# Where a matrix's operand words are cut in the queue of a seven-product gated MLP kernel

## The chip, the cores and the metric

The kernel runs on one core of one Trainium2 chip. The metric is the device time of one execution in microseconds (us); the kernel before takes 1533.95 us, the median of three runs.

## The reference

The program normalises `x` (2048 x 576), runs a linear attention on it and a gated MLP beside it, and returns `x + s * silu(MLP)`. The change touches only the first part of the MLP:

```python
def _B_ref(x, w_gate, w_up, w_down):
    g = jnp.einsum("bsd,df->bsf", x, w_gate)      # 2048 x 576 x 4608
    u = jnp.einsum("bsd,df->bsf", x, w_up)
    h = _gelu(g) * u
    return jnp.einsum("bsf,fd->bsd", h, w_down)
```

All arrays are float32.

## The kernel before, in words

The two products with `w_gate` and `w_up` are cut into 36 *matrices*, q = 0 to 35. An even q is a block of 256 columns of `w_gate`, an odd q the same columns of `w_up`; the two together are called a pair here. Each matrix is a 2 x 2 block product done with seven products instead of eight. `STEPS` lists them in the order in which TensorE (PE) does them: k = 0 to 6 with the weights A11, S1, S3, S2, A12, S4, A22. S1 to S4 are sums of the four weight blocks: S1 = A21 + A22, S2 = S1 - A11, S3 = A11 - A21, S4 = A12 - S2. GpSimd (POOL) makes all four per matrix in `mat_sums`, into the tile `sm`.

Every product is done for two halves s of the tokens, s = 1 first. Float32 accuracy comes from two float32r words per value, so each sum and each raw block is cut into words: `cut_w` has ScalarE (ACT) copy the high word and then VectorE (DVE) subtract it twice (the low word of 2 x 128 rows, then that of a group of 32 rows). In the profile these are ACT `wa<-sm`, `wb<-raw` and so on at L104, and two DVE subtractions of the same names at L107. `wa` holds the words of A11, S1, S2, S3, `wb` those of A12, A22, S4.

The products add into PSUM banks named `al`, `ga`, `de`, `be`; (k - q) % 4 chooses the bank, so the next matrix takes each bank over in turn: `be` of matrix q+1 takes the bank of `de` of matrix q, `al` that of `be`, `ga` that of `al`, `de` that of `ga`. PE works on four groups of 32 rows, each group running some steps behind the group before it, so PE starts a bank of the next matrix about 3.5 us after the last matmul of this matrix into that bank. In between, DVE or ACT must have read it out.

The order on DVE, ACT and POOL is the order in which the program is written; an instruction that waits holds all behind it on its engine. `roll` emits the matmuls, and behind the last of a step (q, k, s) it calls `matrix(...)`'s `step`, which reads the bank. Behind step k with s = 0 it runs the list `todo[k]`. That list comes from `mat_pieces(q + 1)`, so the words of the next matrix are cut in the shadow of this one:

```python
            if s == SBS[-1]:
                run(todo[k])
```

An up matrix (odd q) multiplies the hidden tile `h` by what the banks give (DVE) and has POOL make eight sums of hidden blocks (`hs`, `h`) that go to DRAM. A gate matrix (even q) passes each block through a Gelu on ACT, and `down_sums` behind its k = 3 has POOL make four sums of the down weights (`td`). POOL takes up the four sums `sm` for the next matrix behind step k = 0.

The MLP's second part (`down_all`, L1068), the attention before it and all loads stay as they are.

Of the kernel before, what the change touches and what calls it, by code (L numbers as in the profile page):

```python
# [57 lines left out]
def group(t):  # L58
    return slice(t * KR, (t + 1) * KR)
# [6 lines left out]
def block_kernel(ctx, tc, x, xe, xt_d, wq_d, wkv0_d, wkv1_d, wkv2_d, wo, wgu_d, wd_d, out):  # L66
# [22 lines left out]
    def mid(i, shape, dt, name):  # L89
        return sb.tile(shape, dt, tag=f"m{i}", bufs=1, name=name)  # L90
# [12 lines left out]
    def act(*args, **kw):  # L103
        pin(nc.scalar.activation(*args, **kw))  # L104

    def vec(op, *args, **kw):
        pin(getattr(nc.vector, op)(*args, **kw))  # L107
# [6 lines left out]
    def pool(op, *args, **kw):  # L114
        pin(getattr(nc.gpsimd, op)(*args, **kw))
# [370 lines left out]
    def run(todo, n=None):  # L486
        for _ in range(len(todo) if n is None else min(n, len(todo))):
            todo.pop(0)()
# [243 lines left out]
    def s_mm(tb, t):  # L732
# [15 lines left out]
        if t == 0:  # L748
# [6 lines left out]
    raw, sums, wt = {}, {}, {}  # L755
# [3 lines left out]

    W_AT = {"A11": ("a", 0), "S1": ("a", 1), "S2": ("a", 2), "S3": ("a", 3),
            "A12": ("b", 1), "S4": ("b", 3)}

    def w_at(q, nm):
        t, i = ("b", 2 if q % 2 == 0 else 0) if nm == "A22" else W_AT[nm]
        return wt[t][:, i]

    def load_mat(q):
        if q < NQ:  # L770
            raw[q] = mid(0, [P, 2, 3, 2 * P], F32, f"raw_{q}")
            dma(out=raw[q], in_=wgu_d[q // 2, q % 2])

    def mat_sums(q):
        if q >= NQ:
            return
        rv = raw[q].rearrange("p j k (f c) -> p j f k c", f=2)
        a11, a21, a12, a22 = rv[:, 0, 0], rv[:, 0, 1], rv[:, 1, 0], rv[:, 1, 1]
        sm = mid(2, [P, 4, 3, P], F32, f"sm_{q}")
        pool("tensor_add", sm[:, 0], a21, a22)  # L780
        pool("tensor_sub", sm[:, 1], sm[:, 0], a11)
        pool("tensor_sub", sm[:, 2], a11, a21)
        pool("tensor_sub", sm[:, 3], a12, sm[:, 1])
        sums[q] = rv, sm

    def cut_w(o, src, nm):

        r = group(W_LO[nm])
        act(o[:, :, 0:3, :], src, AF.Copy)
        vec("tensor_sub", o[:, :, 3:5, :], src[:, :, 0:2, :], o[:, :, 0:2, :].bitcast(F32))  # L790
        vec("tensor_sub", o[r, :, 2, :], src[r, :, 2, :], o[r, :, 2, :].bitcast(F32))

    def mat_pieces(q):

        if q >= NQ:
            return [[] for _ in range(7)]
        rv, sm = sums.pop(q)
        if q % 2 == 0:
            raws_ = [lambda: cut_w(wt["b"][:, 1:3], rv[:, 1], "A12")]
        else:  # L800
            raws_ = [
                lambda: cut_w(wt["b"][:, 1:2], rv[:, 1, 0:1], "A12"),
                lambda: cut_w(wt["b"][:, 0:1], rv[:, 1, 1:2], "A22"),
            ]
        return [
            [lambda: cut_w(wt["a"][:, 0:1], rv[:, 0, 0:1], "A11")],
            [], [],
            [lambda: cut_w(wt["a"][:, 1:4], sm[:, 0:3], "S1")],
            raws_,
            [lambda: cut_w(wt["b"][:, 3:4], sm[:, 3:4], "S4")],  # L810
            [],
        ]

    STEPS = (
# [570 lines left out]
    def back(*names, eng=nc.gpsimd):  # L1385
        for nm in names:
            X[0][nm] = big(X_BACK[nm], [P, 5, TBN], F32R, f"xr_{nm}")
            dma(X[0][nm].bitcast(F32), store[0, nm], eng)

    def first_matrix():  # L1390
        wt["a"] = big(15, [P, 4, 5, P], F32R, "wa")
        return mat_pieces(0)
# [11 lines left out]
        (3, 2): [lambda: scale(0, 2, 3, 4), lambda: halve(0, 2, 3, 4)],  # L1404
        (3, 3): [lambda: build(1, "T4", X_SLOT["T4"]), lambda: back("T2")],
        (0, 0): [lambda: den(1), lambda: mat_sums(0)],
        (0, 1): [lambda: scale(1, 0, 1), lambda: halve(1, 0, 1)],
        (0, 2): [lambda: scale(1, 2, 3, 4), lambda: halve(1, 2, 3, 4)],
        (0, 3): [lambda: back("T1")],
        (1, 0): [lambda: pieces.extend(first_matrix()), lambda: run(pieces[0])],  # L1410
        (1, 1): [lambda: run(pieces[3])],
    }
    pieces = []
    for tb in (2, 3, 0, 1):
# [2 lines left out]
            run(aside.get((tb, t), []))  # L1417
    wt["b"] = big(14, [P, 4, 5, P], F32R, "wb")
    back("T3")
    run(pieces[4] + pieces[5])  # L1420
    load_mat(1)
    back("B21", "B22", "T4", eng=nc.sync)

    def matrix_of(q):

        g = q // 2
        mat_sums(q + 1)
        todo = mat_pieces(q + 1)
        if q % 2 == 0:
            todo[0].append(lambda: load_down(g))  # L1430
            todo[3].append(lambda: down_sums(g))
        todo[4].append(lambda: load_mat(q + 2))
        if q == NQ - 1:
            load_s(3)
            todo[0].append(lambda: load_t(1))
            todo[2].append(lambda: prep_t(1))
            todo[3] += [lambda: load_t(2), lambda: prep_s(1)]
            todo[4].append(lambda: prep_s(2))
            todo[4].append(lambda: load_s(5))
            todo[5].append(lambda: load_t(3))  # L1440
            todo[6].append(lambda: prep_s(3))
        return (gate_matrix if q % 2 == 0 else up_matrix)(g, todo)
# [59 lines left out]
```

## Time and profile before

| | before |
|---|---|
| runs, us | 1533.95, 1532.64, 1534.01 |
| profiled execution, us | 1536.59 |
| its span, us | 1534.5 |
| PE busy | 1484.4 us, 97% |
| DVE busy | 1063.6 us, 69% |
| ACT busy | 604.9 us, 39% |
| POOL busy | 548.1 us, 36% |
| 333 to 1112 us (the pairs): PE, DVE, POOL busy | 740.4, 589.9, 398.8 of 779.0 us |

The granted TensorE clock is 0.997 over the span, and 1.00 in the stretch of the pairs. In a row of the profile the first number is the start in us, the second the length, then engine, line, operation, out<-in, shapes; what stands in square brackets is the engine's idle time before the instruction and what ended it. Names lack their numbers, so `u<-u,de` is the DVE sum of `u` and the bank `de` for whichever matrix and half.

### The profile page before, as it was taken

How to read it: one execution, taken by the hardware profiler on the slowest of the kernel's cores; microseconds unless marked ns; L12 is line 12 of the kernel's file. 1: busy time of each engine (PE TensorE's matmuls, PEld its weight loads, DVE VectorE, ACT ScalarE, POOL GpSimd, SP SyncE). 2: the span in 40 equal slices, each digit the busy share in tenths (PEclk: the TensorE clock that was granted, in tenths of full speed). 3: DMA queues.
4: the chain of work that ended last, by engine and by line, in shares of the span. 5: the costliest groups of instructions: out<-in, count | busy, mean ns of one | idle time of the engine just before them, and what ended most of it. 6: DMA issues, size and time to landing. Idle time of an engine off the chain costs nothing.

```text
span 1534.5 us, 42454 instructions
## 1 busy us (share of the span) xinstructions
PE 1484.4 (97%) x18431; PEld 1392.7 (91%) x18431; DVE 1063.6 (69%) x1579; ACT 604.9 (39%) x1119; POOL 548.1 (36%) x520
## 2 busy tenths in 40 slices
PE   9999999999999999999999999999999999999998
PEld 8989989988888888888889888889889999999998
DVE  7676567277778777778777778777684666555775
ACT  5444455333332233332233332233334545444443
POOL 5452521144565544565544565544410020000120
PEclk9999999999999999999999999999989999999999
DMA  6354015633344333344423443423577757787773
GB/s 231 128 219 163 1 52 193 247 126 117 135 170 164 140 120 115 142 170 150 153 103 125 150 169 145 156 99 123 211 286 245 255 169 249 245 267 250 277 244 126
DMA packets 114548, 261.96 MB, mean 171 GB/s; under 512 B 10218, under 2 KB 38634, under 8 KB 112314
## 3 DMA queue, kind: packets, MB, share of 16 engines
q1 hardware_dynamic: 112586, 249.95, 46.0%
q0 software_dynamic: 1632, 8.91, 1.6%
q8 instruction: 144, 2.36, 0.7%
q14 instruction: 42, 0.34, 0.1%
q10 hardware_dynamic: 144, 0.39, 0.1%
HBM read 161.27 MB, written 97.91 MB: 169 GB/s over the span
## 4 chain that ended last, share of the span: by engine, by line
PE 70%; DVE 25%; issue 2%; ACT 1%; DMA 1%; SPq 0%; ACTq 0%
PE bd L1068 26%; PE be L110 9%; DVE h L107 8%; PE kv L110 7%; PE de L110 7%; PE al L110 7%; DVE wb L107 7%; DVE u L107 6%; PE ga L110 5%; PE s L110 3%; PE q L110 3%; DVE wa L107 3%; PE kv_a L110 1%; ACT wa L104 1%; DMA x<-in_xe_dram 0%
## 5 line engine op out<-in xcount | busy, mean ns | idle before, releaser
L1068 PE MATMUL bd<-t,s 128*128 128x288 f32 x3024 | 405.6, 296 | 3.5 <-DVE u L107 3.5
L1068 PEld LDWEIGHTS bd<-t,s 128*128 128x128 f32 x3024 | 404.8, 189 | 4.5 <-DVE u L107 4.1
L110 PE MATMUL be<-xo_T,wa 32*128 32x512 f32 x972 | 248.0, 389 | 28.6 <-DVE u L107 28.6
L110 PE MATMUL de<-xo_T,wa 32*128 32x512 f32 x972 | 255.9, 393 | 10.0 <-DVE h L107 9.9
L107 DVE TENSOR_TENSOR s<-sr,s 128x512 fp32r<-128x512 f32 x252 | 176.0, 739 | 125.0 <-ACT s L104 120.5
L110 PE MATMUL al<-xr_B,wa 32*128 32x512 f32 x972 | 256.6, 391 | 0.0
L110 PE MATMUL ga<-xr_T,wa 32*128 32x512 f32 x972 | 252.4, 390 | 0.0
L110 PE MATMUL ga<-xo_T,wa 32*128 32x512 f32 x972 | 252.4, 390 | 0.0
L110 PE MATMUL de<-xr_T,wb 32*128 32x512 f32 x972 | 248.9, 387 | 0.0
L110 PE MATMUL de<-xr_T,wa 32*128 32x512 f32 x972 | 246.9, 387 | 0.0
L110 PE MATMUL be<-xr_T,wa 32*128 32x512 f32 x972 | 245.4, 386 | 0.0
L110 PE MATMUL al<-xo_B,wa 32*128 32x512 f32 x972 | 245.1, 386 | 0.0
L110 PE MATMUL ga<-xr_B,wb 32*128 32x512 f32 x972 | 244.0, 385 | 0.0
L110 PE MATMUL de<-xo_T,wb 32*128 32x512 f32 x972 | 243.4, 384 | 0.0
L110 PE MATMUL al<-xo_B,wb 32*128 32x512 f32 x972 | 243.4, 384 | 0.0
L110 PE MATMUL al<-xr_B,wb 32*128 32x512 f32 x972 | 243.1, 384 | 0.0
L110 PE MATMUL ga<-xo_B,wb 32*128 32x512 f32 x972 | 243.0, 384 | 0.0
L104 ACT ACTIVATE s<-sr 128x512 fp32r<-128x512 f32 x252 | 148.7, 625 | 195.7 <-PE bd L1068 149.1
L110 PEld LDWEIGHTS be<-xo_T,wa 32*128 32x128 f32 x972 | 175.1, 183 | 46.9 <-DVE u L107 35.8
L110 PEld LDWEIGHTS de<-xo_T,wa 32*128 32x128 f32 x972 | 172.6, 183 | 22.1 <-DVE h L107 17.2
L110 PEld LDWEIGHTS be<-xr_T,wa 32*128 32x128 f32 x972 | 176.4, 183 | 10.9 <-DVE u L107 5.5
L110 PEld LDWEIGHTS de<-xr_T,wa 32*128 32x128 f32 x972 | 176.4, 183 | 5.6
(177 smaller groups left out, 4318.6 us busy)
## 6 DMA issues: line engine op xcount, KB each, us to landing
sr<-hs SPq DMA_DIRECT2D x252, 256.0 KB
hs<-h SPq DMA_DIRECT2D x68, 512.0 KB
raw<-in_wgu_dram SPq DMA_DIRECT2D x36, 768.0 KB
hs<-hs SPq DMA_DIRECT2D x102, 256.0 KB
td<-in_wd_dram SPq DMA_DIRECT2D x18, 576.0 KB
td<-td SPq DMA_DIRECT2D x18, 576.0 KB
tr<-td SPq DMA_DIRECT2D x16, 576.0 KB
tr<-in_wd_dram SPq DMA_DIRECT2D x12, 576.0 KB
```

The lines of the kernel that those rows point to most:

```text
L104: pin(nc.scalar.activation(*args, **kw))
L107: pin(getattr(nc.vector, op)(*args, **kw))
L110: i = nc.tensor.matmul(*args, **kw)
L1068: nc.tensor.matmul(banks[j][:, 0:HALF], hw[n, s][:, a, t * P : (t + 1) * P], w[:, c, g % 4], start=(new and g == 0 and m == 0), stop=(g == ...
```

## The change

The words of S1 and S3 are cut behind the third product (k = 2) and no longer behind the fourth; those of S2 stay behind the fourth (k = 3), now alone; those of S4 go from behind the sixth (k = 5) to behind the last (k = 6). So that S1 and S3 lie side by side, S3 and S2 change places in `wa` and in `sm`, and POOL makes S3 before S2.

```diff
-    W_AT = {"A11": ("a", 0), "S1": ("a", 1), "S2": ("a", 2), "S3": ("a", 3),
+    W_AT = {"A11": ("a", 0), "S1": ("a", 1), "S3": ("a", 2), "S2": ("a", 3),
...
         pool("tensor_add", sm[:, 0], a21, a22)
-        pool("tensor_sub", sm[:, 1], sm[:, 0], a11)
-        pool("tensor_sub", sm[:, 2], a11, a21)
-        pool("tensor_sub", sm[:, 3], a12, sm[:, 1])
+        pool("tensor_sub", sm[:, 1], a11, a21)
+        pool("tensor_sub", sm[:, 2], sm[:, 0], a11)
+        pool("tensor_sub", sm[:, 3], a12, sm[:, 2])
...
             [lambda: cut_w(wt["a"][:, 0:1], rv[:, 0, 0:1], "A11")],
-            [], [],
-            [lambda: cut_w(wt["a"][:, 1:4], sm[:, 0:3], "S1")],
+            [],
+            [lambda: cut_w(wt["a"][:, 1:3], sm[:, 0:2], "S1")],
+            [lambda: cut_w(wt["a"][:, 3:4], sm[:, 2:3], "S2")],
             raws_,
-            [lambda: cut_w(wt["b"][:, 3:4], sm[:, 3:4], "S4")],
             [],
+            [lambda: cut_w(wt["b"][:, 3:4], sm[:, 3:4], "S4")],
```

The first matrix, whose words are cut ahead of `roll`, takes its pieces by the new numbers (`pieces[2] + pieces[3]`, `pieces[4] + pieces[6]`); the order there is the same.

DVE's queue at the end of an up matrix (q = 11; `wb<-sm` are the words of S4 for matrix 12, `u_1`, `u_0` with `de` the reading of the last product). Before:

```order
L107 TENSOR_TENSOR u_5_0_8434<-u_0_8124,ga_0_8009 128x512
L107 TENSOR_TENSOR h_0_1_7655<-h_0_1_7655,u_5_0_8434 128x512
L107 TENSOR_TENSOR wb<-sm_8088,wb 128x256
L107 TENSOR_TENSOR wb<-sm_8088,wb 32x128
L107 TENSOR_TENSOR u_1_8093<-u_1_8093,de_1_8040 128x512
L107 TENSOR_TENSOR h_1_0_7652<-h_1_0_7652,u_1_8093 128x512
L107 TENSOR_TENSOR u_0_8124<-u_0_8124,de_0_8071 128x512
L107 TENSOR_TENSOR h_0_0_7654<-h_0_0_7654,u_0_8124 128x512
L107 TENSOR_TENSOR wa<-raw_8363,wa 128x256
```

Now:

```order
L107 TENSOR_TENSOR u_5_0_8473<-u_0_8160,ga_0_8042 128x512
L107 TENSOR_TENSOR h_0_1_7688<-h_0_1_7688,u_5_0_8473 128x512
L107 TENSOR_TENSOR u_1_8129<-u_1_8129,de_1_8073 128x512
L107 TENSOR_TENSOR h_1_0_7685<-h_1_0_7685,u_1_8129 128x512
L107 TENSOR_TENSOR u_0_8160<-u_0_8160,de_0_8107 128x512
L107 TENSOR_TENSOR h_0_0_7687<-h_0_0_7687,u_0_8160 128x512
L107 TENSOR_TENSOR wb<-sm_8124,wb 128x256
L107 TENSOR_TENSOR wb<-sm_8124,wb 32x128
L107 TENSOR_TENSOR wa<-raw_8402,wa 128x256
```

The two subtractions of S4 have gone behind the four instructions that read `de`.

DVE's queue in the middle of a gate matrix (q = 12; `wa<-sm` are the words for matrix 13, `u_1`, `u_0` with `be` the reading of the fourth product, `wb<-raw` the words of the next A12). Before:

```order
L107 TENSOR_TENSOR h_0_1_8555<-h_0_1_8555,de_0_8526 128x512
L107 TENSOR_TENSOR u_1_8556<-u_1_8556,be_1_8566 128x512
L107 TENSOR_TENSOR h_1_1_8553<-h_1_1_8553,u_1_8556 128x512
L107 TENSOR_TENSOR u_0_8587<-u_0_8587,be_0_8598 128x512
L107 TENSOR_TENSOR h_0_1_8555<-h_0_1_8555,u_0_8587 128x512
L107 TENSOR_TENSOR wa<-sm_8547,wa 128x3x256
L107 TENSOR_TENSOR wa<-sm_8547,wa 32x3x128
L107 TENSOR_TENSOR wb<-raw_8363,wb 128x256
```

Now:

```order
L107 TENSOR_TENSOR h_0_1_8594<-h_0_1_8594,de_0_8565 128x512
L107 TENSOR_TENSOR wa<-sm_8586,wa 128x2x256
L107 TENSOR_TENSOR wa<-sm_8586,wa 32x2x128
L107 TENSOR_TENSOR u_1_8595<-u_1_8595,be_1_8605 128x512
L107 TENSOR_TENSOR h_1_1_8592<-h_1_1_8592,u_1_8595 128x512
L107 TENSOR_TENSOR u_0_8626<-u_0_8626,be_0_8637 128x512
L107 TENSOR_TENSOR h_0_1_8594<-h_0_1_8594,u_0_8626 128x512
L107 TENSOR_TENSOR wa<-sm_8586,wa 128x256
L107 TENSOR_TENSOR wa<-sm_8586,wa 32x128
L107 TENSOR_TENSOR wb<-raw_8402,wb 128x256
```

Two of the three sums' words now stand ahead of the reading of `be`, as two instructions of their own; up matrices change in the same way. DVE and ACT have 72 and 36 rows more in all; SP's and PE's queues are in the same order as before.

More of the change, by code (lines that the diff above doesn't have):

```diff
@@ L806, in mat_pieces @@
             [lambda: cut_w(wt["a"][:, 0:1], rv[:, 0, 0:1], "A11")],
-            [], [],
-            [lambda: cut_w(wt["a"][:, 1:4], sm[:, 0:3], "S1")],
+            [],
+            [lambda: cut_w(wt["a"][:, 1:3], sm[:, 0:2], "S1")],
+            [lambda: cut_w(wt["a"][:, 3:4], sm[:, 2:3], "S2")],
             raws_,
+            [],
             [lambda: cut_w(wt["b"][:, 3:4], sm[:, 3:4], "S4")],
-            [],
         ]
@@ L1410, in block_kernel @@
         (1, 0): [lambda: pieces.extend(first_matrix()), lambda: run(pieces[0])],
-        (1, 1): [lambda: run(pieces[3])],
+        (1, 1): [lambda: run(pieces[2] + pieces[3])],
     }
@@ L1419, in block_kernel @@
     back("T3")
-    run(pieces[4] + pieces[5])
+    run(pieces[4] + pieces[6])
     load_mat(1)
```

## The prediction

> **What bounds the kernel now.** I read the page first, then PE's waits, and then the timelines of one pair, engine by engine. PE is busy 97% of the span, so only its idle time can be won, and PE's waits between 325 and 1112 us, where the pairs run, name all of that but refill:
>
> ```profile
> PE be L110 <- DVE u L107: 28.6, 17, 1.7
> PE de L110 <- DVE h L107: 9.9, 16, 1.2
> ```
>
> Two waits repeat, once a pair: 1.7 us before `be` of a gate matrix and 0.6 us on average before `de` of an up matrix. The pair of matrices 12 (gate) and 13 (up) stands for the rest. First PE, two rows of its timeline, the first matmuls of two neighbouring steps:
>
> ```profile
> 565.83 0.38 PE L110 MATMUL de<-xr_T,wa 32*128 32x512 f32 x1
> ...
> 569.30 0.49 PE L110 MATMUL be<-xo_T,wa 32*128 32x512 f32 x1 [1.66 <-DVE u L107]
> ```
>
> This step takes 3.47 us. A step without a wait takes 1.48 (2.95 for two, from the rows at 581.85 and 584.80 below), so the stall costs 2.0, some 0.3 more than its gap. What DVE did before it:
>
> ```profile
> 553.16 0.69 DVE L107 TENSOR_TENSOR u<-u,de 128x512 f32<-128x512 f32 x1 [0.90 <-PE de L110]
> 554.47 0.69 DVE L107 TENSOR_TENSOR u<-u,be 128x512 f32<-128x512 f32 x1 [0.61 <-PE be L110]
> ...
> 558.58 1.52 DVE L107 TENSOR_TENSOR wa<-sm,wa 128x768 fp32r<-128x768 f32 x2
> ...
> 561.33 1.12 DVE L107 TENSOR_TENSOR wb<-raw,wb 128x512 fp32r<-128x512 f32 x2
> ...
> 564.53 1.28 DVE L107 TENSOR_TENSOR h<-h,u 128x512 f32<-128x512 f32 x1
> 565.73 2.79 DVE L107 TENSOR_TENSOR wb<-sm,wb 128x256 fp32r<-128x256 f32 x2
> 568.55 0.69 DVE L107 TENSOR_TENSOR u<-u,de 128x512 f32<-128x512 f32 x1
> ```
>
> The words of S4 (565.73) hold DVE for 2.79 us, and `u<-u,de` behind them ends at 569.24, just before PE goes on at 569.30. This is the stall. The same two subtractions take 0.73 at 590.42 (below). The difference is POOL, which makes its `hs` sums from before 565 until 575.75: a DVE instruction whose inputs are both in SBUF stretches there (`h<-h,u`: 1.28 instead of 0.69), one that reads a bank does not (568.55: 0.69). Now the gate half on DVE, ACT, POOL and PE:
>
> ```profile
> 576.76 0.69 DVE L107 TENSOR_TENSOR h<-h,de 128x512 f32<-128x512 f32 x1 [0.67 <-PE de L110]
> 578.30 0.69 DVE L107 TENSOR_TENSOR u<-u,be 128x512 f32<-128x512 f32 x1 [0.84 <-PE be L110]
> 579.02 1.34 DVE L107 TENSOR_TENSOR h<-h,u 128x512 f32<-128x512 f32 x1
> 580.28 0.67 DVE L107 TENSOR_TENSOR u<-u,be 128x512 f32<-128x512 f32 x1
> 580.99 0.69 DVE L107 TENSOR_TENSOR h<-h,u 128x512 f32<-128x512 f32 x1
> 583.44 2.04 DVE L107 TENSOR_TENSOR wa<-sm,wa 128x768 fp32r<-128x768 f32 x2 [1.75 <-ACT wa L104]
> 585.49 2.50 DVE L107 TENSOR_TENSOR wb<-raw,wb 128x256 fp32r<-128x256 f32 x4
> 588.02 1.29 DVE L107 TENSOR_TENSOR h<-u,ga 128x512 f32<-128x512 f32 x2
> 590.42 0.73 DVE L107 TENSOR_TENSOR wb<-sm,wb 128x256 fp32r<-128x256 f32 x2 [1.11 <-ACT wb L104]
> ```
>
> ```profile
> 559.28 0.85 ACT L104 ACTIVATE wb<-raw 128x768 fp32r<-128x768 f32 x1 [1.98 <-PE al L110]
> ...
> 581.72 0.63 ACT L104 ACTIVATE h<-h 128x512 f32<-128x512 f32 x1 [0.69 <-DVE h L107]
> 582.25 1.15 ACT L104 ACTIVATE wa<-sm 128x1152 fp32r<-128x1152 f32 x1
> 583.31 1.06 ACT L104 ACTIVATE h<-al 128x512 f32<-128x512 f32 x2
> 584.26 0.94 ACT L104 ACTIVATE wb<-raw 128x384 fp32r<-128x384 f32 x2
> ```
>
> ```profile
> 576.85 1.02 POOL L115 TENSOR_TENSOR sm<-sm,raw 128x384 f32<-128x384 f32 x1
> 577.81 1.02 POOL L115 TENSOR_TENSOR sm<-raw 128x384 f32<-128x384 f32 x1
> 578.79 1.02 POOL L115 TENSOR_TENSOR sm<-raw,sm 128x384 f32<-128x384 f32 x1
> 582.76 4.34 POOL L115 TENSOR_TENSOR td<-td 128x288 f32<-128x288 f32 x4 [2.95 <-DMA td<-in_wd_dram]
> ```
>
> ```profile
> 581.85 0.38 PE L110 MATMUL al<-xo_B,wa 32*128 32x512 f32 x1
> ...
> 584.80 0.38 PE L110 MATMUL ga<-xo_T,wa 32*128 32x512 f32 x1
> ...
> 588.76 0.49 PE L110 MATMUL de<-xo_T,wa 32*128 32x512 f32 x1 [0.57 <-DVE h L107]
> ```
>
> The second wait: `h<-u,ga` (588.02) queues behind seven word instructions, which ran beside the four `td` sums. And POOL's sums come late in a gate matrix, where they queue behind `hs`: the second of them ends at 577.87, the last at 579.81, when the matrix's fourth product is already being read (578.30).
>
> **The change part by part.** *S4 behind the last product.* In the up half 2.79 us go from ahead of `u<-u,de`, so it runs at 565.73 to 566.42. PE's slot for `be` is at 565.83 + 1.5 = 567.3: no stall. Its second half is ready at about 566.4 + 1.3 (`h<-h,u`, stretched) + 0.7 = 568.4, against a slot at 568.8. The S4 words follow, at the same price, and DVE comes out of them and A11's words at the same time as before. S4 is next read two steps before the end of the next matrix, so nothing waits for them. Gain: 2.0 a pair, if nothing else comes late. In the gate half there is no such gain: S4's words stand idle time away from `h<-u,de` (1.11 at 590.42, waiting for ACT) and only change places with it.
>
> *S1 and S3 behind the third product, up half.* DVE is idle 0.61 before `u<-u,be` (554.47). ACT starts when the last reading of the third product can (553.16) and takes 0.85 for 768 elements, so DVE cuts from 554.05 for 1.12 (the row at 561.33 has the same shapes), and `be` is read at 555.2, 0.7 later than now. The bank has 3.5 us. Behind it S2 alone costs 0.73 and not 1.52, so the queue is back in step at `h<-h,al` to within 0.1, and POOL starts its sums when it did.
>
> *The same, gate half.* Here the cover is missing. ACT can copy S1 and S3 only when POOL has made S3, its second sum, at 577.87. That time does not move: POOL's chain from the first `hs` sum on is set by the up half. ACT then has the copies at 577.93 + 0.85 = 578.8, and the words on DVE begin, beside POOL's fourth sum. Free they would take 1.12 and end at 579.9. By the row at 579.02, which ran beside that same sum and ended 0.55 behind it, the first ends at 580.3 and the second (0.42) at 580.7. I take 580.7, since the shapes and the neighbour are the same; the ends of the range are 579.9 and, by the 2.04 at 583.44, 580.9. Behind them stands `u<-u,be`: 580.7 to 581.4 and not 578.30. PE, 2.0 us earlier now, wants that bank for `al` of matrix 13 at 581.85 - 2.0 = 579.85 and gets it at 581.45. So 1.6 of the 2.0 comes back as a wait of PE's `al` for DVE's `u`.
>
> Then `h<-h,u`, `u<-u,be` and `h<-h,u` follow. The last starts at 582.85, beside the first `td` sum (582.76, a quarter of 4.34 at most), and ends between 583.55 (free) and 584.4; I take 584.0, as one stretched instruction, against 581.68 now. ACT's second Gelu follows it, S2's copy (about 0.5 instead of 1.15, from 0.94 for two at 584.26), then the reading of `al`. Now that reading's first half ends 2.12 behind the Gelu's start (583.31 + 0.53 - 581.72, with half of 1.06); with the shorter copy that is 1.5. So 584.0 + 0.05 + 1.5 = 585.6, and `ga` of matrix 13, which wants this bank at 581.45 + 2.95 = 584.4, waits until then; it now starts at 584.80. Two steps later, at 588.6 to 588.9, comes `de`. DVE must have read `ga` by then: S2's copy at 585.1, then its words 0.73 to 1.3, the four of `wb<-raw` 1.5 to 2.5, 0.69 for `h<-u,ga`: 588.0 to 589.6, nearest 588.8, since part of the `td` sums is over. `de` started at 588.76 before. The pair is therefore even at this point, between -0.4 and +0.5. Two smaller terms speak for a gain: the wait at `de` gets shorter, so that refill behind it, about 0.3 a stall, is partly paid earlier and inside the other waits (-0.2), and the up half's 0.1. I take +0.1 - 0.2 - 0.05 = -0.15 a pair.
>
> *The split itself.* Each matrix has one ACT and two DVE instructions more. By the rows that is 1.12 + 0.73 - 1.52 = 0.33 on DVE, 34 x 0.33 = 11 us, all of it in idle time in the up half and within the sums above in the gate half.
> The Trainium skill speaks against the split (Perfetto Trace Analysis, "Optimizing Scalar/DVE Operations": each DVE instruction on SBUF has about 60 ns of overhead). By that it would be an estimated 0.12 a matrix, 4 us in all; the row says nearly three times as much, and I go by the row.
>
> *The sum.* 17 pairs have the first wait. 17 x -0.15 = -2.6. On the profiled execution, 1536.59 with a span of 1534.5, this gives 1534.0; that execution is 2.6 above the median of the runs. From the median, 1533.95 - 2.6 = 1531.
>
> **The rivals.** *The stall goes and none replaces it.* 17 x 2.0 = 34 us, 1500. For it: DVE is idle 0.61 to 0.90 before every `be` and `de` reading, and the three-sum words shrink just where `de` waits. Against it: the idle time before 578.30 ends 0.5 us before the S1 and S3 copies can exist. It would need their words done by 579.1.
> This is what the Trainium skill's rule would make of it (same page and section: where Scalar and Vector aren't saturated but cause bubbles elsewhere, breaking up instructions may let work complete sooner); the trace agrees for the up half only.
>
> *The late words decide, slower.* One mechanism: in the gate half the words of S1 and S3 end later than 581.0, or the last `h<-h,u` is stretched to 584.4, and everything behind (Gelu, reading of `al`, S2's words, four `wb` words beside `td`, `h<-u,ga`) is pushed along. Nothing between can give time back. From `h<-u,ga` ending beyond 589.0 each pair is slower. At the upper ends, 589.6 against 588.71 now, it is 0.9 less 0.3 for the terms above, so +0.6 a pair, 17 x 0.6 = 10 us, 1544. For it: DVE instructions beside POOL often take the longer of two values (558.58: 1.52, 583.44: 2.04). Against: a part of the `td` sums is over by then.
>
> *It does nothing*, the order being set elsewhere: the queues show that it moves, so this has little.
>
> **How the numbers follow.** Forecast 0.53, with its own range -0.45 to +0.25 a pair, 1526 to 1538. Late words, slower, 0.33. Stall gone 0.11. Nothing 0.03. About 0.2% (3 us) is what a measurement can tell from no change. Of the forecast, 0.25 lies below -3 us, 0.23 within, 0.05 above. With 0.11 the chance of faster is 0.36; with 0.03 and a small end of the late words (0.03) that of the same is 0.29; slower is 0.05 + 0.30 = 0.35. The range takes in the forecast and the slower rival and leaves out the stall that goes altogether: 1523 to 1545.
>
> **What would show it.** Right: PE's waits list no `be` after DVE `u` any more, but `al` after DVE `u`, 17 times about 1.6 us, and perhaps `ga` after ACT `h`; in the gate half DVE shows idle time before `wa<-sm` of about 2 us, ended by ACT, ahead of `u<-u,be`; `de` after `h` is smaller. In each pair POOL starts its first `hs` sum as long after the pair before as now. Wrong: no new wait of 1 us or more (then the time is near 1500), a `be` wait that is still there, or `sm` sums that come earlier.

## The result, and the profile after

| | before | after |
|---|---|---|
| median, us (12 runs each) | 1533.98 | 1531.39 |
| lowest to highest, us | 1532.36 to 1538.70 | 1528.08 to 1536.54 |
| profiled execution, us | 1536.59 | 1536.36 |

The ratio is 0.9985 with a 95% interval of 0.9970 to 0.9999: 2.6 us less, as in the prediction's sum. That agreement is closer than the measurement, whose interval runs from 0.2 to 4.6 us. The two profiled executions hide even this, and the windows of both, here up to the pairs, say why. The columns are the busy time and instructions of PE, of its weight load, of DVE, ACT and POOL, then the granted clock, the DMA share and GB/s; before first, then after:

```profile
0.00:330.00 330.00, 326.50 (x2545) 308.63 (x2545) 207.53 (x418) 156.22 (x369) 116.11 (x150) 1.00 0.40 148
```

```profile
0.00:330.00 330.00, 325.94 (x2455) 307.54 (x2459) 202.51 (x415) 155.42 (x370) 115.80 (x150) 0.98 0.40 148
```

The profiled execution of after had a lower clock ahead of the pairs, where the change moves nothing, and did 90 matmuls fewer in that time. So the pairs are to be measured from a mark of their own: the first of the `hs` sums that POOL makes as PE takes up a pair (they belong to the hidden blocks of the pair before). Here are the marks of the second pair (matrices 2 and 3) and of the seventeenth, on POOL's timeline of before and of after:

```profile
333.10 1.29 POOL L115 TENSOR_TENSOR hs<-h,h 128x512 f32<-128x512 f32 x1 [13.33 <-DVE h L107]
...
1026.65 1.29 POOL L115 TENSOR_TENSOR hs<-h,h 128x512 f32<-128x512 f32 x1 [13.11 <-DVE h L107]
```

```profile
338.10 1.29 POOL L115 TENSOR_TENSOR hs<-h,h 128x512 f32<-128x512 f32 x1 [12.99 <-DVE h L107]
...
1029.62 1.29 POOL L115 TENSOR_TENSOR hs<-h,h 128x512 f32<-128x512 f32 x1 [13.01 <-DVE h L107]
```

Fifteen pairs took 693.55 us before (1026.65 - 333.10) and 691.52 after: 0.135 less a pair, against the 0.15 forecast. Single pairs of before differ by more than that: they took 45.78 to 46.81 us. PE's waits of after in the stretch of the pairs (total, times, longest):

```profile
PE ga L110 <- ACT h L104: 14.5, 23, 2.0
PE al L110 <- DVE u L107: 14.3, 14, 1.4
PE de L110 <- DVE h L107: 5.5, 14, 0.6
```

The `be` wait (28.6 us before) is gone. Two others stand in its place, and `de` is smaller (9.9 before). The `al` wait comes in 14 of the 17 pairs. The pair of matrices 12 and 13 again, now with POOL's first `hs` sum at 568.27 (563.97 before). PE's timeline, the two steps of the old stall and the three new starts:

```profile
570.16 0.39 PE L110 MATMUL de<-xr_T,wa 32*128 32x512 f32 x1
...
571.75 0.38 PE L110 MATMUL be<-xo_T,wa 32*128 32x512 f32 x1
...
585.68 0.50 PE L110 MATMUL al<-xo_B,wa 32*128 32x512 f32 x1 [1.33 <-DVE u L107]
...
589.29 0.49 PE L110 MATMUL ga<-xo_T,wa 32*128 32x512 f32 x1 [0.33 <-ACT h L104]
...
593.16 0.49 PE L110 MATMUL de<-xo_T,wa 32*128 32x512 f32 x1 [0.37 <-DVE h L107]
```

The step before `be` takes 1.59 and no longer 3.47. The gate half on DVE, with ACT's first copy of the new words and the first three of POOL's four sums, is where it goes:

```profile
583.07 1.84 DVE L107 TENSOR_TENSOR wa<-sm,wa 128x512 fp32r<-128x512 f32 x2 [2.70 <-ACT wa L104]
584.94 0.69 DVE L107 TENSOR_TENSOR u<-u,be 128x512 f32<-128x512 f32 x1
...
586.99 0.69 DVE L107 TENSOR_TENSOR h<-h,u 128x512 f32<-128x512 f32 x1
588.79 1.52 DVE L107 TENSOR_TENSOR wa<-sm,wa 128x256 fp32r<-128x256 f32 x2 [1.11 <-ACT wa L104]
590.33 2.06 DVE L107 TENSOR_TENSOR wb<-raw,wb 128x256 fp32r<-128x256 f32 x4
```

```profile
582.19 0.85 ACT L104 ACTIVATE wa<-sm 128x768 fp32r<-128x768 f32 x1 [2.76 <-POOL sm L115]
```

```profile
580.17 1.98 POOL L115 TENSOR_TENSOR sm<-raw 128x384 f32<-128x384 f32 x2
582.12 1.01 POOL L115 TENSOR_TENSOR sm<-sm,raw 128x384 f32<-128x384 f32 x1
...
587.31 3.74 POOL L115 TENSOR_TENSOR td<-td 128x288 f32<-128x288 f32 x4 [2.68 <-DMA td<-in_wd_dram]
```

POOL has S1 and S3 at 582.15, ACT copies them at once, DVE stands idle 2.70 us ahead of their words, and the reading of `be` behind them frees PE's `al` bank at 585.63; PE starts it at 585.68.

### The profile page after: what moved, and what is told of

The parts are those of the page before. It is cut to its first block, busy times and chain, and to the rows that moved or that the text cites. A ratio compares the mean times of both kernels' runs of the same rounds, so it can differ in the third digit from the quotient of the medians.

```text
span 1534.6 us, 42632 instructions
## 1 busy us (share of the span) xinstructions
PE 1489.4 (97%) x18431; PEld 1395.8 (91%) x18431; DVE 1074.2 (70%) x1651; ACT 614.6 (40%) x1155; POOL 548.0 (36%) x520
## 4 chain that ended last, share of the span: by engine, by line
PE 50%; issue 16%; DVE 14%; POOL 12%; DMA 4%; ACT 3%; POOLq 0%; ACTq 0%; SPq 0%; DVEq 0%
PE bd L1069 26%; PE kv L110 7%; POOL sm L115 5%; POOL hs L115 5%; DVE h L107 4%; PE de L110 4%; PE s L110 3%; DVE wa L107 3%; POOL h L115 3%; DVE u L107 3%; PE ga L110 3%; PE al L110 2%; DMA raw<-in_wgu_dram 2%; DVE wb L107 2%; PE q L110 2%
## 5 line engine op out<-in xcount | busy, mean ns | idle before, releaser
L110 PE MATMUL al<-xo_B,wa 32*128 32x512 f32 x972 | 254.1, 394 | 14.3 <-DVE u L107 14.3
L110 PE MATMUL ga<-xr_B,wb 32*128 32x512 f32 x972 | 253.5, 393 | 8.7 <-ACT h L104 8.6
L110 PE MATMUL de<-xo_T,wa 32*128 32x512 f32 x972 | 246.9, 389 | 5.5 <-DVE h L107 5.5
L110 PE MATMUL al<-xr_B,wb 32*128 32x512 f32 x972 | 252.1, 390 | 0.0
L110 PE MATMUL de<-xo_T,wb 32*128 32x512 f32 x972 | 249.1, 388 | 0.0
L110 PE MATMUL ga<-xr_T,wa 32*128 32x512 f32 x972 | 246.7, 389 | 0.0
L110 PEld LDWEIGHTS al<-xo_B,wa 32*128 32x128 f32 x972 | 175.6, 185 | 24.9 <-DVE u L107 20.2
L110 PEld LDWEIGHTS ga<-xo_T,wa 32*128 32x128 f32 x972 | 177.4, 186 | 17.4 <-ACT h L104 12.5
L110 PEld LDWEIGHTS de<-xo_T,wa 32*128 32x128 f32 x972 | 177.8, 184 | 16.0 <-DVE h L107 11.8
L110 PEld LDWEIGHTS ga<-xr_B,wb 32*128 32x128 f32 x972 | 174.1, 184 | 19.3 <-ACT h L104 14.7
```

The source lines that it names most:

```text
L110: i = nc.tensor.matmul(*args, **kw)
```

## The experiments

Ten kernels were run. "Gate half" means words cut during a gate matrix (for the up matrix that follows), "up half" the reverse. All ratios are to the kernel before on the same chip, with 95% intervals.

| S4 | S1, S3 early | other | median, us | ratio |
|---|---|---|---|---|
| as before | both halves | | 1532.92 | 0.9991 (0.9979 to 1.0003) |
| last | no | | 1510.73 | 0.9847 (0.9828 to 0.9866) |
| last in up half | no | | 1512.69 | 0.9857 (0.9831 to 0.9882) |
| last | up half | | 1515.06 | 0.9872 (0.9851 to 0.9893) |
| last | both halves | weights' sums first | 1539.16 | 1.0032 (1.0021 to 1.0044) |
| last | both halves | the same, `td` load ahead | 1506.23 | 0.9806 (0.9777 to 0.9835) |
| last | no | `td` sums in up matrix | 1491.84 | 0.9717 (0.9695 to 0.9738) |
| last | both halves | `td` sums in up matrix | 1524.20 | 0.9927 (0.9905 to 0.9948) |
| last | both halves | both of these | 1506.87 | 0.9813 (0.9786 to 0.9841) |
| last | up half | `td` sums in up matrix | 1494.96 | 0.9738 (0.9718 to 0.9758) |

### S4's move alone

```diff
             raws_,
-            [lambda: cut_w(wt["b"][:, 3:4], sm[:, 3:4], "S4")],
             [],
+            [lambda: cut_w(wt["b"][:, 3:4], sm[:, 3:4], "S4")],
```

> The kernel before with S4's words behind the last product and nothing else changed: S1, S2 and S3 stay together behind the fourth. My theory (the early S1/S3 words of the gate half take back what S4's move gives): the be wait goes and no wait of al for DVE's u comes. In the gate half the three sums exist by about 14.9 us after POOL's first hidden sum, before the words are asked for, so PE keeps nearly its own pace: 46.2 us a pair becomes 43.0 to 44.0, 17 x -2.2 to -3.2, so 1480 to 1497, say 1490. First rival (DVE is full beside POOL, a pair cannot be shorter than 46 whatever the order): another DVE wait comes instead and the time stays at 1528 to 1534. Second rival (the early S1/S3 words are what thins out the de wait, so without them it grows): the de wait rises from 0.6 to about 2 a pair and the time is 1510 to 1525.

It gained 24 us (from 1534.58 on its chip), more than the whole change and less than expected. Six of sixteen pairs took 43.8 to 44.0 us, as expected; the average was 44.8, against 46.25 before. PE's waits of this kernel:

```profile
PE de L110 <- DVE h L107: 14.5, 17, 1.5
PE ga L110 <- ACT h L104: 7.5, 7, 1.7
```

No `be` and no `al`: without the early words the up matrix is not held at its first product. But `de` went from 9.9 to 14.5 us, since PE, earlier by 2 us, comes upon the same words beside the `td` sums. One pair (its first `hs` sum is at 557.15), POOL and DVE:

```profile
557.15 1.29 POOL L115 TENSOR_TENSOR hs<-h,h 128x512 f32<-128x512 f32 x1 [11.57 <-DVE h L107]
...
576.34 3.52 POOL L115 TENSOR_TENSOR td<-td 128x288 f32<-128x288 f32 x4 [2.23 <-DMA td<-in_wd_dram]
```

```profile
569.41 0.69 DVE L107 TENSOR_TENSOR u<-u,be 128x512 f32<-128x512 f32 x1 [0.16 <-PE be L110]
...
575.92 3.22 DVE L107 TENSOR_TENSOR wb<-raw,wb 128x256 fp32r<-128x256 f32 x4
```

The four `wb` words take 3.22 us beside `td`, and `de` waits behind them. The expectation missed this step. The same move in the up half only, where the forecast had put all its gain:

```diff
-            [lambda: cut_w(wt["b"][:, 3:4], sm[:, 3:4], "S4")],
-            [],
+            [lambda: cut_w(wt["b"][:, 3:4], sm[:, 3:4], "S4")] if q % 2 else [],
+            [] if q % 2 else [lambda: cut_w(wt["b"][:, 3:4], sm[:, 3:4], "S4")],
```

> The kernel before with S4's words behind the last product in up matrices only; in gate matrices they stay behind the sixth. My theory: the whole gain of S4's move comes from the up half, where the words are stretched by the hidden sums; the time is that of S4's move alone, 1507 to 1514. Rival (the gate half has a share): 1516 to 1530.

1512.69, with an interval that overlaps the former: in the time, the gate half's S4 is worth nothing that can be told from no change. The traces show 0.2 us a pair (see the small terms below).

### The early words alone, and in the up half only

S4 as before, S1 and S3 early:

```diff
-            [],
             [lambda: cut_w(wt["b"][:, 3:4], sm[:, 3:4], "S4")],
+            [],
```

> The changed kernel with S4's words back behind the sixth product: only S1 and S3 are moved. My theory: the be wait of 1.7 a pair is back, and since PE is then 2 us later, the reading of be behind the S1/S3 words comes in time for al, so al no longer waits; from there on the pair goes by the same POOL sums, and ga and de start within 0.2 us of where they do in the changed kernel. Time as the kernel before to within 3 us: 1531 to 1537. First rival (pair time is set by DVE's work alone): the same 1531 to 1537 but with al waiting too. Second rival (the early words help by themselves, by emptying the fourth step): de no longer waits and the time is 1515 to 1525.

1532.92, as expected. PE's waits of this kernel have `be` as before and no `al`:

```profile
PE be L110 <- DVE u L107: 29.9, 17, 1.8
PE de L110 <- DVE h L107: 2.1, 5, 0.6
PE ga L110 <- ACT h L104: 1.7, 5, 0.4
```

So the early words bring no wait at `al` while PE comes 2 us later to it: the old stall is what covered them. They do thin out the `de` wait (9.9 us before), and the time hardly shows it. All runs of this kernel had a granted clock of 0.990 to 0.995 and those of before 0.995 to 0.999, so a gain of a few us may be hidden here. Now the changed kernel with the early words in the up half only:

```diff
-            [lambda: cut_w(wt["a"][:, 1:3], sm[:, 0:2], "S1")],
+            [lambda: cut_w(wt["a"][:, 1:3], sm[:, 0:2], "S1")] if q % 2 == 0 else [],
...
```

(q is here the matrix that the words are for; for odd q, in the gate half, all three are cut behind k = 3, as before).

> The changed kernel, but S1 and S3 are cut behind the third product only while an up matrix runs, where their sums are ready long before; in gate matrices all three sums are cut behind the fourth as before. S4 behind the last everywhere. My theory: the early words cost nothing where the sums are ready, so this is within 3 us of S4's move alone, about 1490 (1480 to 1497), with neither a be nor an al wait. Rival (the early words cost by standing ahead of the be reading, wherever): about half of the loss stays, 1508 to 1515. Rival (DVE full): 1528 to 1534.

1515.06: a miss of the expected 1480 to 1497, since S4's move alone is itself at 1510.73, and next to the 1508 to 1515 of the first rival. The waits tell the two apart: `al` and `be` wait no more, as expected, and `de` waits 18.0 us. The changed kernel lies 16.3 us above, and the one difference is the gate half's early words. That settles the place. The time is also 4.3 us above S4's move alone, with intervals that overlap.

### Is it POOL's S3 sum? The weights' sums first

In the changed kernel the hidden block's third sums and the transfers behind them are put off until POOL has made the weights' four sums:

```diff
-                sum_("tensor_sub", sm[s][2], h1[:, 1], sm[s][1])
-                dma(out=d[:, 0:2], in_=h1, eng=eng)
...
+                def third():
+                    sum_("tensor_sub", sm[s][2], h1[:, 1], sm[s][1])
+                    dma(out=d[:, 0:2], in_=h1, eng=eng)
...
+                held.append(third)
...
         mat_sums(q + 1)
+        run(held)
+        held.clear()
```

> The changed kernel with one change on POOL: the last two hidden sums of an up matrix (one for each half, and the transfers behind them) come behind the four weight sums of the next matrix, not ahead of them. S3's sum is then ready about 2.6 us earlier, some 11.3 us after POOL's first hidden sum instead of 13.9. My theory: it is POOL's late S3 sum that holds DVE ahead of be in the gate half; the al wait (1.4 a pair) and the ga wait behind it shrink to under 0.5 together, and the time falls to 1485 to 1505, say 1495. First rival (the words themselves are too long beside POOL, or DVE is full): the waits move elsewhere and the time stays at 1526 to 1534. Second rival (the hidden sums that now come later hold something): a wait of ACT or POOL for DMA grows and the time is above 1534.

1539.16, slower than before: the expectation missed by 44 us. PE's waits of this kernel have no `al`, so that part held, but three kinds of `ga`, of which this is the largest:

```profile
PE ga L110 <- ACT u L104: 16.2, 11, 2.4
```

SP's queue and ACT, in one pair:

```profile
581.35 1.32 SPq L118 DMA_DIRECT2D hs<-hs  x2
582.72 0.56 SPq L118 DMA_DIRECT2D td<-in_wd_dram  x1
592.79 0.32 SPq L118 DMA_DIRECT2D td<-td  x1
593.22 0.50 SPq L118 DMA_DIRECT2D raw<-in_wgu_dram  x1
```

```profile
598.24 0.52 ACT L104 ACTIVATE wa<-raw 128x384 fp32r<-128x384 f32 x1 [5.64 <-DMA raw<-in_wgu_dram]
```

The put-off transfers hold the load of the down weights, so the `td` sums are late, so their transfer out is late, and behind that stands the load of the next weights, for whose first copy ACT waits 5.64 us; the reading of a bank queues behind that copy. The cure of that is to issue the load ahead of the held transfers:

```diff
         mat_sums(q + 1)
+        if q % 2 == 0:
+            load_down(g)
         run(held)
...
         if q % 2 == 0:
-            todo[0].append(lambda: load_down(g))
```

> The kernel with the weight sums first, and the load of the down weights issued ahead of the transfers that were put off, so that it isn't stuck behind them in SP's queue. What I now think of the run before it: the al wait went because S3's sum came in time (al started 15.9 us after POOL's first hidden sum, on PE's pace), but the td load landed 4 us later, the td sums with it, and the load of the next raw matrix waited behind the td transfer in SP's queue, which held ACT and gave the wait of ga for ACT's u. If so, that wait (16.2 us in all) goes, no al wait comes back, and the time is 1490 to 1515, say 1500. Rival (it was the later hidden sums or DVE's load, not SP's order): ga still waits for ACT's u and the time stays at 1530 to 1540.

1506.23, within the range, 25 us below the changed kernel. The `al` wait is 0.3 us in all. One pair, POOL and DVE:

```profile
558.75 1.29 POOL L115 TENSOR_TENSOR hs<-h,h 128x512 f32<-128x512 f32 x1 [12.95 <-DVE h L107]
...
567.91 2.22 POOL L115 TENSOR_TENSOR sm<-raw 128x384 f32<-128x384 f32 x2
```

```profile
571.05 1.85 DVE L107 TENSOR_TENSOR wa<-sm,wa 128x512 fp32r<-128x512 f32 x2
572.93 0.69 DVE L107 TENSOR_TENSOR u<-u,be 128x512 f32<-128x512 f32 x1
```

POOL has S3 11.38 us behind its first `hs` sum, against 13.88 in the changed kernel (582.15 - 568.27), and the reading of `be` starts 14.18 us behind it, against 16.67 (584.94 - 568.27): both 2.5 us earlier, although the words themselves still take 1.85 us. The late S3 sum is shown to be the cause of the `al` wait.

### The down weights' sums

S4's move alone, and POOL's four `td` sums made in the up matrix that follows (in the last pair they stay in the gate matrix):

```diff
         if q % 2 == 0:
             todo[0].append(lambda: load_down(g))
-            todo[3].append(lambda: down_sums(g))
+        if q % 2 == (g < NG - 1):
+            todo[0 if q % 2 else 3].append(lambda: down_sums(g))
```

> S4's words behind the last product with S1, S2 and S3 together behind the fourth, and besides POOL's four td sums moved from behind the fourth product of a gate matrix to behind the first of the up matrix, where DVE has idle time. My theory: the de wait that S4's move alone leaves (14.5 us in 17 waits, with refill about 1.2 us a pair) is DVE's words of A12 and A22 stretched by the td sums beside them; it goes, and the time is 1488 to 1498, say 1492. Rival (the words are late by themselves, since ACT must copy them behind two Gelus): de still waits, 1506 to 1512. Rival (the td sums now stretch DVE's reading of the up matrix's fourth product instead): another wait and 1505 or more.

1491.84, the fastest of all, 42 us below before. The `de` wait fell from 14.5 us to 0.4, and the same four words on DVE take 1.47:

```profile
PE ga L110 <- ACT h L104: 7.4, 8, 1.8
...
PE de L110 <- DVE h L107: 0.4, 1, 0.4
```

```profile
570.63 1.47 DVE L107 TENSOR_TENSOR wb<-raw,wb 128x256 fp32r<-128x256 f32 x4
```

The same edit to the changed kernel:

> The changed kernel with the td sums moved in the same way, to behind the first product of the up matrix. My theory: the al wait (1.4 a pair) stays, since POOL's S3 sum is as late as it was, and ga still waits for ACT behind the late reading of be; only the words of S2, A12 and A22 get shorter, so de no longer waits: 0.3 to 0.7 a pair, 1519 to 1527, say 1522. Rival (the td sums, not the S3 sum, are what holds the gate half): al and ga waits go too, and the time is 1490 to 1505.

1524.20, 7.2 less than the changed kernel. Its `al` wait is untouched, as it must be if POOL's S3 sum sets it:

```profile
PE al L110 <- DVE u L107: 15.3, 14, 1.4
PE ga L110 <- ACT h L104: 12.7, 23, 1.8
PE de L110 <- DVE h L107: 0.4, 1, 0.4
```

So with `td` out of the way the gate half's early words cost 1524.20 - 1494.96 = 29 us; the second number is that of the run that follows, which has the early words in the up half alone:

> S4 behind the last product in all matrices, S1 and S3 early only where an up matrix's words are not concerned with POOL's queue (the words for the next gate matrix), and the four down-weight sums in the up matrix. Without the last it ran 1515.1, 4.3 above S4's move alone. My theory: those 4.3 us are the wait of de beside the down-weight sums, 23.5 us behind POOL's first hidden sum in every pair instead of 22.6 in some; with these sums away it is at 22.0 as with S4's move alone, and the time is that of S4's move with the sums moved, 1491.8: 1490 to 1494. The rival: the early words cost something in the up half itself; then the 4.3 us stay, 1495 to 1498.

1494.96 lies between the two expectations. It is 3.1 above S4's move with the same edit, with intervals that overlap; whether the up half's early words cost those 3 us or nothing stays open. They are not a gain.

Last, the changed kernel with both cures:

> The changed kernel with both cures together: the weights' four sums go ahead of the hidden block's third sums and transfers on POOL (and the load of the down weights ahead of those transfers), and the four down-weight sums go into the up matrix. My theory: the gate half of the change loses to POOL in two places, the second sum S3, for which al of the up matrix waits, and the down-weight sums, beside which DVE makes the words ahead of de. With the first cured alone it ran 1506.2, with the second alone 1524.2. With both, al starts 16.2 us behind POOL's first hidden sum as in the first cure, and de 5.9 to 6.2 us later (on PE's pace) instead of 6.9, so 0.7 to 1 us a pair less than 1506: 1490 to 1498, and PE lists no al and no de wait. The rival: the early words cost by themselves, since they are 72 instructions more on DVE and stand ahead of the reading of be; then it stays at 1502 or above, with waits for DVE left in the list.

1506.87, a miss: no better than the first cure alone, and the rival's number, though of the rival's waits for DVE only 1.5 us are left in the pairs. `al` waits no more and `de` once, nearly as expected, yet `ga` is left:

```profile
PE ga L110 <- ACT h L104: 10.9, 19, 1.8
...
PE ga L110 <- DVE h L107: 1.1, 2, 0.8
PE de L110 <- DVE h L107: 0.4, 1, 0.4
```

Of the 15 us to the fastest kernel (12 to the one with early words in the up half alone) I can name no single place. The early words still run beside POOL's sums (1.85 us, as in the first cure), and the held transfers leave the hidden tile later. The two were not told apart.

## Why the prediction was right

**The stall goes.** Right: 1.59 instead of 3.47 a step is 1.9 a pair of the 2.0 taken.

**The gate half's cover is missing.** Right in its cause, shown by the kernel with the sums first, and in its times. Behind POOL's first `hs` sum the words were to end at 580.7 - 563.97 = 16.7 and PE's `al` to start at 17.5. They ended at 16.64 (583.07 + 1.84) and it started at 17.41. In S4's move alone `al` starts where PE's pace puts it,

```profile
573.03 0.38 PE L110 MATMUL al<-xo_B,wa 32*128 32x512 f32 x1
```

15.88 behind its mark, so the words cost 1.53 there, against 1.6. The list shows 1.33 in this pair and 1.0 on average, 14 times and not 17: where PE has been held earlier in the pair (below, under what I did not name), it comes to `al` later and waits there less or not at all.

**The last `h<-h,u` stretched, then `ga`.** Mis-sized. It was to end 20.0 behind the mark; it ran in 0.69 and ended at 19.41 (586.99 + 0.69 - 568.27), although the first `td` sum began beside it at 587.31. So `ga` started 21.02 behind the mark and not 21.6.

**`de` is even.** Right, by two misses that cancel, which is luck: the 0.6 came back in S2's words, 1.52 us beside `td` where I had 0.73 to 1.3. `de` started 24.89 behind the mark; 24.8 was expected, and it was 24.79 before. (The prediction counts seven word instructions ahead of `h<-u,ga`; its rows show six, which changes nothing in its sum.) The Trainium skill has the mechanism (SBUF — State Buffer, "Who interferes with whom": a VectorE instruction with two SBUF inputs contends with a GpSimd one that reads SBUF). The trace agrees: the four `wb` words took 3.22 us beside the sums and 1.47 without, while a reading of a bank beside POOL's sums (568.55 before) kept its 0.69.

**The small terms.** The whole forecast gain lies behind `de`: 0.2 for refill and 0.05 for the up half. The size was right, by luck; the reason for the 0.2 was wrong. Over sixteen pairs, `de` starts 24.93 behind the mark (24.81 before), and from there to the next mark PE needs 21.17 us, against 21.44: 0.27 less. But before, this stretch took 21.42 to 21.47 in every pair, whether `de` had waited 1.15 us or had no wait in the list, so a shorter `de` wait gives nothing there. It took 21.42 on average with S4 last in the up half only, and 21.22 with S4 last in both halves. So the 0.2 is S4's move in the gate half, where the prediction saw no gain. That fits the queue: `be` of the up matrix takes the bank that `h<-u,de` reads, and S4's words no longer stand ahead of that reading.

**What I did not name.** Of the 14.5 us of `ga` waits, 8.6 belong to another step, the sixth product of the gate matrix: ACT's copy of `ga` into the hidden tile waits for a transfer out of that tile. In one pair of the changed kernel, ACT and PE:

```profile
903.38 0.60 ACT L104 ACTIVATE h<-ga 128x512 f32<-128x512 f32 x1 [5.74 <-DMA hs<-h]
```

```profile
904.03 0.49 PE L110 MATMUL ga<-xr_B,wb 32*128 32x512 f32 x1 [1.90 <-ACT h L104]
```

ACT's waits for this, before and after:

```profile
ACT h L104 <- DMA hs<-h: 18.8, 14, 2.4
```

```profile
ACT h L104 <- DMA hs<-h: 50.1, 14, 5.7
```

A PE that comes 2 us earlier meets the transfer. In the changed kernel this costs little: `al` starts 17.39 to 17.43 behind the mark in 13 of 16 pairs, with that wait or without it, and the eight pairs that have it took 46.13 us on average, the other eight 46.08. In S4's move alone nothing covers it: the seven pairs that have it took 45.57, the other nine 44.21. That makes an estimated 7 x 1.36 = 10 us of the 20 by which this kernel missed its expected 1490. It is read from the pairs and not shown by an experiment: no run has a larger ring of hidden tiles, which would test it.

**The rival that the stall simply goes** was priced at 34 us, 2.0 a pair. Without the early words S4's move gives 24, as other waits take the stall's place; its shortest pairs took 43.82 us, 2.4 less than the average before (46.25). With the `td` sums moved as well it gives 42.

## What to carry to other kernels

A stall covers work behind it. Before taking it away, list for each queue what now runs into its shadow; here S3's sum, the `td` sums and a transfer out did, in that order. An operand that another engine makes late is not to be cut early, and an instruction that waits for it must not stand ahead of the reading of a bank.

## What the runs showed of the hardware

A stall costs more than its listed gap. From the pairs on, PE's waits of before sum to 42.0 us (28.6, 9.9 and 3.5 at the start of the second part), those of the fastest kernel to 9.1 (7.4, 0.4 and 1.3), yet the spans differ by 45.6 us (1534.5 and 1488.9). Of the missing 13, PE's busy time holds 12, for as many matmuls (18431):

```profile
sum 1540.00, PE 1484.39 PEld 1392.65 DVE 1063.60 ACT 604.91 POOL 548.14; mean PE 494.80 PEld 464.22 DVE 354.53 ACT 201.64 POOL 182.71
```

```profile
sum 1540.00, PE 1472.40 PEld 1421.04 DVE 1037.62 ACT 608.75 POOL 549.31; mean PE 490.80 PEld 473.68 DVE 345.88 ACT 202.92 POOL 183.10
```

(windows up to 1540 us, before and the fastest.) As I read it, a group of 32 rows that waits while the other three run counts as busy; no run takes that apart. The list of waits showed under three quarters of what there was to win, so the prediction's premise that only PE's idle time can be won does not hold.

The place of one load in SP's queue, behind the put-off transfers or ahead of them, was worth 33 us (1539.16 and 1506.23). A few of these may be the clock's, granted at 0.990 to 0.994 in the runs of the first and at 0.995 to 0.998 in those of the second.
